# Fused attention and mixture of experts: a new order of the attention periods, fixed PSUM places, the k and q casts cut in two, one score block in fp32

## Chip, core and metric

The kernel is one program on one core of a Trainium2 chip. The metric is the device time of one execution in microseconds (us). The engines are TensorE (PE in the profile; its weight loads are the row PEld), VectorE (DVE), ScalarE (ACT), GpSimd (POOL) and SyncE (SP, which here only starts transfers). Line numbers such as L228 are lines of the kernel before.

## What is computed

Block-causal attention over 8 batches of 8 heads, then a two-level router and 16 experts. All of it is fp32 in and out.

```python
def _attn_ref(q, k, v):                       # q, k, v: (8, 8, 576, 64)
    scores = scale * np.matmul(q, k.transpose(0, 1, 3, 2))
    mask = (pos[:, None] // 64) >= (pos[None, :] // 64)
    scores = np.where(mask, scores, -1000000000.0)
    scores = scores - np.max(scores, axis=-1, keepdims=True)
    attn = np.exp(scores)
    attn = attn / (np.sum(attn, axis=-1, keepdims=True) + 1e-09)
    return np.matmul(attn, v)
...
def _moe_ref(x, w_group, w_expert, w1, w2):   # x: (4608, 512), 4 groups of 4 experts, F = 1024
    g_idx = argmax(x @ w_group); g_w = softmax(x @ w_group)[g_idx]
    e_idx = argmax(x @ w_expert[g_idx]); e_w = softmax(...)[e_idx]
    out = g_w * e_w * (relu(x @ w1[g, e]) @ w2[g, e])
```

## The kernel before

**Attention.** The 64 heads are taken as 32 pairs. A pair's work is a set of tokens, each a few instructions: `K` transposes k and q on PE into a PSUM tile (L157), `k0` and `k1` copy 512 columns each of it to SBUF (`nf`) on ACT; the last 64 columns of k and 128 of q (64 of them padding, "the tails") come through three more transposes (L175) into the free part of another pair's `o` tile, and `j0`, `j1` copy them to `nf` on DVE. `h0`, `h1` cast `nf` to fp32r (the high part), `l0`, `l1` subtract it from `nf` (the low part): both lie in `qk`, k in columns 0 to 575, q in 576 to 1215. A score tile is then three fp32r products, high by high, high q by low k, low q by high k (`PROD`), for each head of the pair. `S0` to `S3` and `S8` are the score tiles of 128, 256, 384, 512 and 576 columns (L228, L218; L234 adds the mask), and the 128-column one lies in the same PSUM tile as the 384-column one, behind it (`S2`). `D` takes the row maximum (DVE, L239), `E` the exponential (ACT, L251), `T` transposes the result back (PE, L157), `t` copies that to `pt` (ACT, L284), `V` multiplies with v in fp32 (PE, L313) and ends with the tail transposes of a later pair, and `v` copies its result out (DVE, L281).

**The software pipeline.** `period(x)` walks the table `ORDER`, in which `S1@0` is token `S1` of pair x, `K@-1` token `K` of pair x+1, and so on; a `d` behind it puts it on DVE, an `a` on ACT. There are 31 such periods and one that walks `END`. The program order of each engine is the order of the tokens; nothing is scheduled afterwards. The router's tokens (`R`, `L`, `n`, `Y`, `M`, `X`, `G`, `Z`) act once in four periods, for the batch that the last four pairs have completed: `L`, `Y`, `X` are PE work (logits and transposes), `n0`, `n1` copies on ACT, `M` and `G` DVE, `Z` indirect DMAs on POOL that write x and its weights. Hooks, given by a token's position or by a step, place the other POOL work.

**PSUM.** Every tile of the attention (transposes, scores, results) is a place of 2 x 512 columns, of which there are four, given in turn to whoever asks next:

```python
def wide(self, name):
    return self.ps2.tile([P, 2, 512], F32, tag="W", name=name)   # pool ps2, bufs=4
```

A period asks for ten of them (`K`, `S1`, `S2`, `S3`, `S8`, `T1` to `T4`, `V`), and one to four more where the router has PE work.

**Experts.** From about 345 us on, the 4608 rows are gathered by expert and go through w1 and w2 in slots. `spill` and `overflow` handle rows beyond the planned slots in a loop whose count (`cnti`) is computed on the chip and is zero for these inputs.

Of the kernel before, what the change touches and what calls it, by code (L numbers as in the profile page):

```python
# [8 lines left out]
F32 = mybir.dt.float32  # L9
# [5 lines left out]
ALU = mybir.AluOpType  # L15
# [37 lines left out]
Z2@7 E3@1 S2@0 D2@0 Z4@8 E2@1 n1@3a E8@1 T1@1 t3@1a t1@1a D0@0 K@-1 Z0@10 Y1@4 S3@0 D3@0 G2@6 R0@3  # L53
k0@-1a V@2 k1@-1a E0@0 E4@0 E5@0 E1@0 M1@4 E6@0 T2@1 S1@0 L0@3 E7@0 t2@1a T4@1 Z3@8 G1@5 S8@0 G0@4 j0@-1d G4@6
j1@-1d t0@1a Z1@9 h0@-1a v@2d L1@2 D1@0 l0@-1d D8@0 n0@3a G3@6 X0@4 X1@5 Y0@3 h1@-1a t4@1a M0@3 l1@-1a T3@0
X2@6
# [11 lines left out]
class Attention:  # L68
    def __init__(self, tc, ctx, inner, q, k, v, consts):
# [9 lines left out]
        self.ps2 = self.psx.enter_context(tc.tile_pool(name="ps2", bufs=4, space=PSUM))  # L79
# [124 lines left out]
    def score(self, i, u):  # L204
# [17 lines left out]
        for u, c0 in ((2, 0), (0, 384)) if u == 2 else ((u, 0),):  # L222
            w = P * (u + 1)
            st = r["s", u] = ps[:, :, c0:c0 + w]
            for x, (hq, hk) in enumerate(self.PROD):
                for z in range(2):
                    p = slice(64 * z, 64 * z + 64)
                    nc.tensor.matmul(st[:, z, :], lhsT=t[p, hq, S + P * u:S + P * u + P], rhs=t[p, hk, 0:w],  # L228
                                     start=x == 0 and c0 == 0, stop=False)
        m = 2 if u == 0 else 1  # L230
# [93 lines left out]
    def start(self, N, order, on_dve, init):  # L324
# [45 lines left out]
    def token(self, i, tok, N):  # L370
# [54 lines left out]
class Router:  # L425
# [187 lines left out]
    def spill(self, at, row, cnti):  # L613
# [32 lines left out]
        V.tensor_copy(cnti[0:1, 0:1], g[0:1, 0, R - 1:R])  # L646
        yield

    def token(self, at, b, tok):
# [61 lines left out]
        elif k == "Z":  # L711
            self.scatter(b, st, j, at.gate(at.now, 3) if j == 3 and not at.closed else None)
# [130 lines left out]
class Moe:  # L843
# [302 lines left out]
    def store(self, s, c, full):  # L1146
# [215 lines left out]
def attention_moe(ctx, tc, q, k, v, w_group, w_expert, w1, w2, out, order=None, on_dve=None):  # L1362
# [16 lines left out]
    with tc.manual_schedule(engines={ET.PE, ET.Activation, ET.DVE, ET.Pool, ET.SP}):  # L1379
# [81 lines left out]
        for _ in run:  # L1461
            pass
# [27 lines left out]
```

## Time and profile before

| what | us |
|---|---|
| median of 3 runs (lowest, highest) | 786.12 (785.64, 787.31) |
| the profiled execution | 785.75 |
| its span, first to last instruction | 784.0 |
| PE busy (share of the span) | 759.1 (97%) |
| DVE busy | 544.7 (69%) |
| ACT busy | 500.4 (64%) |
| POOL busy | 350.2 (45%) |

The profiled execution is 1.75 us longer than its span and lies 0.37 us below the median. Matmuls are pipelined and their ends modelled, so that PE's share is an upper figure. The shares are means over a span whose first 345 us are attention with the router and whose rest is experts: the engines' shares differ between them.

### The profile page before, as it was taken

To read this page: it belongs to the slowest core of one execution; us is meant where nothing else is said; L and a number is where in the kernel's file an instruction comes from. 1 tells how busy PE (TensorE), PEld (TensorE's weight loads), DVE (VectorE), ACT (ScalarE), POOL (GpSimd) and SP (SyncE) were. 2 spreads that over 40 slices of the span, in tenths; PEclk is the share of its full clock that TensorE was granted. 3 is DMA by queue.
4 is the path that set the end of the run, shared out by engine and by line. 5 is a ranking of instruction groups with operands and counts; after the bars stand their busy time and mean duration, and the time that the engine had idled before them with its cause. 6 is when DMAs were issued, how large, how long until landed. Compare 5 with 4: busy or idle time off the path is not lost.

```text
span 784.0 us, 20180 instructions
## 1 busy us (share of the span) xinstructions
PE 759.1 (97%) x7422; PEld 620.5 (79%) x7422; DVE 544.7 (69%) x1153; ACT 500.4 (64%) x1244; POOL 350.2 (45%) x481
## 2 busy tenths in 40 slices
PE   7899999999999999999999999999999999999996
PEld 4677777777777787768888788788988888888874
DVE  5567888888888888885454654754666667777742
ACT  5999999999999998755433433432434545545622
POOL 6444345454545454344143644454551553544212
PEclk9999999999999999999999999999999999999999
DMA  6478464646464636443779979979778897787771
GB/s 137 96 210 237 116 137 109 139 109 139 108 139 108 140 102 159 166 123 117 271 203 225 365 228 237 287 223 219 245 200 234 267 268 188 204 250 231 261 245 42
DMA packets 219108, 146.71 MB, mean 187 GB/s; under 512 B 155558, under 2 KB 186870, under 8 KB 219008
## 3 DMA queue, kind: packets, MB, share of 16 engines
q1 hardware_dynamic: 209920, 120.76, 57.6%
q0 software_dynamic: 9088, 24.64, 9.9%
q8 instruction: 60, 0.98, 0.5%
q14 instruction: 40, 0.33, 0.1%
HBM read 113.46 MB, written 24.59 MB: 176 GB/s over the span
## 4 chain that ended last, share of the span: by engine, by line
PE 80%; ACT 7%; DVE 6%; issue 3%; POOL 2%; DMA 2%; POOLq 0%; SPq 0%; ACTq 0%; DVEq 0%
PE h L1050 18%; PE y L1114 18%; PE o L313 10%; PE s L228 7%; PE tp L157 6%; PE h L1043 4%; PE s L218 3%; ACT pb L251 3%; PE ye L1114 3%; ACT pt L284 3%; PE he L1050 3%; PE y L1122 2%; DVE wl L949 1%; PE y L1133 1%; PE lg L690 1%
## 5 line engine op out<-in xcount | busy, mean ns | idle before, releaser
L1050 PE MATMUL h<-xt,wh 128*128 128x264 f32 (+6 forms) x704 | 156.3, 312 | 2.4 <-DVE xt L1010 2.3
L251 ACT ACTIVATE pb<-s,nm 128x128 f32<-128x128 f32 (+4 forms) x288 | 156.1, 568 | 3.5 <-DVE nm L239 1.6
L949 DVE TENSOR_TENSOR wl<-raw,wh 128x512 fp32r<-128x512 f32 x192 | 147.3, 804 | 8.5 <-ACT wh L948 8.4
L239 DVE TENSOR_REDUCE nm<-s 128x2 f32<-128x768 f32 (+4 forms) x160 | 126.3, 806 | 34.1 <-PE s L234 29.9
L1050 PEld LDWEIGHTS h<-xt,wh 128*128 128x128 f32 x704 | 119.2, 188 | 18.2 <-issue 4.2
L948 ACT CAST wh<-raw 128x512 fp32r<-128x512 f32 x192 | 109.6, 618 | 8.6 <-DMA raw<-in_moe_w_dram 6.0
L284 ACT COPY pt<-tp 128x1024 f32<-128x1024 f32 (+4 forms) x160 | 105.3, 696 | 8.6 <-PE tp L157 6.4
L1050 PE MATMUL h<-xt,wl 128*128 128x264 f32 (+6 forms) x352 | 109.2, 310 | 0.0
L1114 PE MATMUL y<-wh,hring 128*128 128x512 f32 x306 | 106.9, 400 | 0.4 <-ACT ys L1165 0.2
L228 PE MATMUL s<-qk 64*128 64x384 f32 (+3 forms) x768 | 89.9, 343 | 6.4 <-POOL qk L199 3.0
L1167 POOL DMA_INDIRECT out_dram<-ys,ids x40 | 47.0, 1174 | 108.1 <-DVE ys L1163 88.3
L313 PE MATMUL o<-pt,vb 128*64 128x320 f32 (+4 forms) x896 | 93.6, 360 | 0.4 <-DVE tmp L708 0.2
L194 POOL CAST qk<-nf 128x640 fp32r<-128x640 f32 (+1 forms) x63 | 42.7, 701 | 98.1 <-DVE nf L281 71.4
L313 PEld LDWEIGHTS o<-pt,vb 128*64 128x64 f32 x896 | 59.3, 137 | 32.2 <-DVE tmp L708 0.3
L157 PE MATMUL tp<-ident,pb 64*128 64x64 f32 x1600 | 76.3, 226 | 1.6 <-DVE xT L281 1.1
L228 PEld LDWEIGHTS s<-qk 64*128 64x128 f32 x768 | 61.6, 188 | 15.0 <-POOL qk L199 6.1
L157 PEld LDWEIGHTS tp<-ident,pb 64*128 64x128 f32 x1600 | 63.8, 140 | 10.2 <-ACT pb L251 3.9
L982 POOL COPY pl<-xg 128x1024 int16<-128x1024 int16 (+3 forms) x35 | 40.3, 1154 | 62.3 <-DMA xg<-xd,ids 40.6
L1114 PEld LDWEIGHTS y<-wh,hring 128*128 128x128 f32 x306 | 57.4, 188 | 13.1 <-DVE hring L1061 0.5
L1050 PEld LDWEIGHTS h<-xt,wl 128*128 128x128 f32 x352 | 66.2, 188 | 1.2
L251 ACT ACTIVATION_READ_ACCUMULATOR pb<-s,nm 128x1 f32 x288 | 64.1, 223 | 0.0
L199 POOL TENSOR_TENSOR qk<-nf,qk 128x640 fp32r<-128x640 f32 x31 | 61.2, 1975 | 2.6
(255 smaller groups left out, 1324.0 us busy)
## 6 DMA issues: line engine op xcount, KB each, us to landing
raw<-in_moe_w_dram SPq DMA_DIRECT2D x96, 512.0 KB, 4.2
rawq<-in_moe_w_dram SPq DMA_DIRECT2D x24, 512.0 KB, 7.8
natk<-in_k_dram SPq DMA_DIRECT2D x32, 256.0 KB, 3.6
natq<-in_q_dram SPq DMA_DIRECT2D x32, 256.0 KB, 5.5
vb<-in_v_dram SPq DMA_DIRECT2D x64, 128.0 KB, 2.8
wh<-in_moe_w_dram SPq DMA_DIRECT2D x16, 512.0 KB, 5.0
xd<-xns SPq DMA_DIRECT2D x12, 512.0 KB, 3.2
tab<-fill POOLq DMA_DIRECT2D x10, 512.0 KB, 4.1
```

What stands on the lines that cost most here:

```text
L157: self.nc.tensor.transpose(out=out[:, z], in_=src[r], identity=self.c["ident"][r, r])
L199: (eng or self.side(("l", n))).tensor_tensor(out=r["qk"][:, 1, o], in0=r["nf"][:, o], in1=r["qk"][:, 0, o].bitcast(F32), op=ALU.subtract)
L228: nc.tensor.matmul(st[:, z, :], lhsT=t[p, hq, S + P * u:S + P * u + P], rhs=t[p, hk, 0:w], start=x == 0 and c0 == 0, stop=False)
L239: self.nc.vector.tensor_reduce(out=o, in_=r["s", u], op=ALU.max, axis=ax, negate=True)
L251: nc.scalar.activation(reg, src, AF.Exp, bias=r["nm"][:, t:t + 1], accum_out=self.sms[b][:, pr, z, u:u + 1])
L284: return self.nc.scalar.copy(dst, src)
L313: nc.tensor.matmul(o[64 * a:64 * a + 64, hf, c0:c0 + BLK * (b1 - t)], lhsT=r["v"][:, a, j, :], rhs=pt[:, PTJ * j + t:PTJ * j + b1, a, :], ...
L948: nc.scalar.copy(h[:, sl], s["raw", u][:, sl])
L949: nc.vector.tensor_tensor(out=l[:, sl], in0=s["raw", u][:, sl], in1=h[:, sl].bitcast(F32), op=ALU.subtract)
L1050: nc.tensor.matmul(o, lhsT=ww[:, dc, f], rhs=rr[:, dc, t], start=dc == 0 and x == 0, stop=dc == 3 and x == 2)
L1114: nc.tensor.matmul(y[c][0:n], lhsT=hh, rhs=w, start=k == 0 and x == 0, stop=k == 7 and x == 2)
L1167: i = nc.gpsimd.indirect_dma_start(out=self.out, out_offset=bass.IndirectOffsetOnAxis(ap=s["ids"][0:n, c, 0:1], axis=0), in_=ys[0:n], in_o ...
```

## The change

1. **Order.** `ORDER` and `END` are new tables. In `ORDER`, `T1` stands behind `V` rather than ahead of `K`; `L0`, `L1` and `Y0`, `Y1` stand ahead of `V` rather than behind it. In `END` all copies are on ACT, where one was on DVE.
2. **PSUM places.** The pool holds four tiles of one place each, `W0` to `W3`, and a string `SLOTS` of 394 digits says for every wide tile which it takes.
3. **Engines.** `t4` (the copy of `T4`, 128 x 640) and `n0` (a router copy, 128 x 576) go from ACT to DVE. The low part of k goes from DVE to POOL.
4. **Casts.** `h0` casts the 512-column mains of k and q in one instruction, `h1` the two tails; `l1` makes q's main low, `l2` the tails' low, `l0` k's main low. All five are on POOL, but for the first pair, where DVE takes part.
5. **Score block.** The 128-column tile `S0` is two fp32 matmuls straight from `nf`, ahead of the 384-column products in their tile, rather than six fp32r matmuls behind them.
6. **Gates, hooks and tail.** Every `Z` waits for the last row maximum by a one-element copy on POOL (before, one of the five did). Hooks move by position. The last slot's result is scaled on ACT alone (512 columns), not on ACT and DVE by halves; the loop's count is copied by POOL behind everything else, not by DVE earlier.

```diff
 ORDER, ON_DVE = parse("""
-Z2@7 E3@1 S2@0 D2@0 Z4@8 E2@1 n1@3a E8@1 T1@1 t3@1a t1@1a D0@0 K@-1 Z0@10 Y1@4 S3@0 D3@0 G2@6 R0@3
...
+E2@1 Z4@10 X0@4 E3@1 S2@0 Z2@7 t3@1a K@-1 E8@1 G0@5 L0@3 k1@-1a L1@3 D2@0 S3@0 k0@-1a n0@3d Y0@4 D0@0 h0@-1a
...
+SLOTS = """
+3210123130210313201302312032102301320312302103201302312032102301301203210230210132103121301231021320123021320231
...
-        self.ps2 = self.psx.enter_context(tc.tile_pool(name="ps2", bufs=4, space=PSUM))
+        self.ps2 = self.psx.enter_context(tc.tile_pool(name="ps2", bufs=1, space=PSUM))
...
-        return self.ps2.tile([P, 2, 512], F32, tag="W", name=name)
+        return self.ps2.tile([P, 2, 512], F32, tag=f"W{next(self.slots)}", name=name)
...
+    def part(self, t, n):
+
+        if n == "kq":
+            return t[:, 0:2 * S].rearrange("p (n c) -> p n c", c=S)[:, :, 0:512]
+        return t[:, dict(k=slice(0, 512), q=slice(S, S + 512), kt=slice(512, S), qt=slice(S + 512, 2 * S + BLK))[n]]
+
+    def high(self, i, n, eng):
         r = self.rs[i]
+        eng.tensor_copy(self.part(r["qk"][:, 0], n), self.part(r["nf"], n))
+
+    def low(self, i, n, eng):
         r = self.rs[i]
+        eng.tensor_tensor(out=self.part(r["qk"][:, 1], n), in0=self.part(r["nf"], n),
+                          in1=self.part(r["qk"][:, 0], n).bitcast(F32), op=ALU.subtract)
...
-        for u, c0 in ((2, 0), (0, 384)) if u == 2 else ((u, 0),):
-            w = P * (u + 1)
...
+        m = 2 if u == 2 else 1
+        if m == 2:
+            st = r["s", 0] = ps[:, :, 384:512]
+            for z in range(2):
+                p = slice(64 * z, 64 * z + 64)
+                nc.tensor.matmul(st[:, z, :], lhsT=r["nf"][p, S:S + P], rhs=r["nf"][p, 0:P], start=True, stop=False)
...
+        self.last_gate = o[0:1, 0:1]
...
-        self.high(0, 0, nc.vector)
-        self.high(0, 1)
-        self.low(0, 0, nc.vector)
-        self.low(0, 1, nc.vector)
+        self.high(0, "k", nc.vector)
+        self.high(0, "q", nc.gpsimd)
+        self.low(0, "k", nc.vector)
+        self.low(0, "q", nc.vector)
+        for n in ("kt", "qt"):
+            self.high(0, n, nc.gpsimd)
+        for n in ("kt", "qt"):
+            self.low(0, n, nc.gpsimd)
...
         elif k == "h":
-            self.high(i, tok[1])
+            for n in ("kt", "qt") if tok[1] else ("kq",):
+                self.high(i, n, self.side(tok))
         elif k == "l":
-            self.low(i, tok[1])
+            for n in (("k",), ("q",), ("kt", "qt"))[tok[1]]:
+                self.low(i, n, self.side(tok))
...
-            self.scatter(b, st, j, at.gate(at.now, 3) if j == 3 and not at.closed else None)
+            self.scatter(b, st, j, None if at.closed else at.last_gate)
...
-            nc.scalar.activation(ys[0:n, 0:256], y[0:n, 0:256], AF.Copy, scale=cw[0:n])
-            nc.vector.tensor_scalar(out=ys[0:n, 256:512], in0=y[0:n, 256:512], scalar1=cw[0:n], scalar2=None, op0=ALU.mult)
+            nc.scalar.activation(ys[0:n], y[0:n], AF.Copy, scale=cw[0:n])
...
+        nc.gpsimd.tensor_copy(cnti, ro.over)
```

What the tables do to the engines' programs is seen in rows of the program order: line, operation, output and inputs (a digit directly behind a name is the pair or the buffer), size, and a count of equal neighbours.

POOL in a period before, pair 12 in buffer 0 and pair 13 in buffer 1 of `qk` and `nf`: two whole casts and the low part of q, with the router's work between two periods.

```order
L194 CAST qk0_113<-nf0_115 128x576
L194 CAST qk0_113<-nf0_115 128x640
L199 TENSOR_TENSOR qk0_113<-nf0_115,qk0_113 128x640
L812 MEMSET mark_200 1x1
L819 DMA tab_57<-pay0_163,pi0_2026 82560x16
L667 COPY ry1_2141<-rx1_2135 128x2x5x2 x2
L194 CAST qk1_114<-nf1_116 128x576
```

POOL in a period of the changed kernel:

```order
L206 CAST qk1_114<-nf1_116 128x2x512
L210 TENSOR_TENSOR qk1_114<-nf1_116,qk1_114 128x512
L206 CAST qk1_114<-nf1_116 128x64
L206 CAST qk1_114<-nf1_116 128x128
L210 TENSOR_TENSOR qk1_114<-nf1_116,qk1_114 128x64
L210 TENSOR_TENSOR qk1_114<-nf1_116,qk1_114 128x128
L210 TENSOR_TENSOR qk1_114<-nf1_116,qk1_114 128x512
```

The first cast of a pair no longer reads its tails; k's low part is now the last instruction here, behind the tails' four small ones.

PE before, from `S2` of pair 13 to `S3`: the 384-column products, the 128-column ones, masks, `T1`, `K` in two rows, `S3`.

```order
L228 MATMUL s13_2_2704<-qk1_114 128x384 x6
L228 MATMUL s13_2_2704<-qk1_114 128x128 x6
L234 LDWEIGHTS mq_121
L234 MATMUL s13_2_2704<-mk_122,mq_121 128x2x64
L234 LDWEIGHTS mq_121
L234 MATMUL s13_2_2704<-mk_122,mq_121 128x2x64
L157 MATMUL tp12_1_2722<-ident_62,pb0_119 128x64 x8
L157 MATMUL tp14_2734<-ident_62,natk0_117 128x64 x8
L157 MATMUL tp14_2734<-ident_62,natq14_2487 128x64 x8
L228 MATMUL s13_3_2753<-qk1_114 128x512 x6
```

PE in the changed kernel, the same stretch of pair 17:

```order
L238 MATMUL s17_2_3553<-nf1_116 128x128 x2
L244 MATMUL s17_2_3553<-qk1_114 128x384 x6
L250 LDWEIGHTS mq_121
L250 MATMUL s17_2_3553<-mk_122,mq_121 128x2x64
L250 LDWEIGHTS mq_121
L250 MATMUL s17_2_3553<-mk_122,mq_121 128x2x64
L164 MATMUL tp18_3565<-ident_62,natk0_117 128x64 x8
L164 MATMUL tp18_3565<-ident_62,natq18_3322 128x64 x8
L244 MATMUL s17_3_3585<-qk1_114 128x512 x6
```

And further on in the same period of the changed kernel, from the end of `V` (L330) past the tail transposes (L182):

```order
L330 MATMUL o15_3597<-pt15_3285,vb_112 64x64 x2
L182 MATMUL o15_3597<-ident_62,natk0_117 128x64 x3
L164 MATMUL tp16_1_3615<-ident_62,pb0_119 128x64 x8
L164 MATMUL tp16_2_3631<-ident_62,pb0_119 128x64 x16
L244 MATMUL s17_1_3650<-qk1_114 128x256 x6
```

The two fp32 matmuls now lead `S2`, and `T1` has moved from ahead of `K` to behind the tail transposes.

DVE before, from `j0` and `j1` of pair 25 to `S2`'s row maximum of pair 24:

```order
L281 COPY nf0_115<-o21_4892 128x64
L282 TENSOR_SCALAR nf0_115<-o21_4892 128x128
L281 COPY xT5_4687<-o21_4892 128x576
L239 TENSOR_REDUCE nm23_4826<-s23_1_4936 128x2
L199 TENSOR_TENSOR qk0_113<-nf0_115,qk0_113 128x576
L239 TENSOR_REDUCE nm23_4826<-s23_8_4960 128x1
```

DVE in the changed kernel at the same place:

```order
L298 COPY nf0_115<-o21_4878 128x64
L299 TENSOR_SCALAR nf0_115<-o21_4878 128x128
L298 COPY xT5_4662<-o21_4878 128x576
L255 TENSOR_REDUCE nm23_4816<-s23_1_4936 128x2
L298 COPY pt22_4763<-tp22_4_4949 128x2x5x64
L255 TENSOR_REDUCE nm23_4816<-s23_8_4963 128x1
```

Between the two row maxima, the subtraction that made k's low part is gone, and the copy of `T4` stands in its place.

## Rows read from the trace of the kernel before

**Rows 1.** Busy time of each engine (instructions) in five periods, from `V` to `V`.

```profile
core 0: us, PE busy (x) PEld busy (x) DVE busy (x) ACT busy (x) POOL busy (x), PEclk, DMA share, GB/s
38.83:48.15 9.32, 8.81 (x138) 6.88 (x134) 5.58 (x9) 9.12 (x26) 4.39 (x6) 1.00 0.55 144
...
117.05:126.37 9.32, 9.32 (x151) 7.49 (x149) 8.24 (x17) 8.77 (x26) 5.60 (x8) 1.00 0.14 45
126.37:135.69 9.32, 9.32 (x154) 7.49 (x150) 8.03 (x17) 9.18 (x27) 4.49 (x6) 1.00 0.62 151
135.69:145.84 10.15, 9.88 (x164) 7.63 (x160) 8.96 (x27) 9.57 (x27) 4.36 (x5) 1.00 0.56 122
145.84:156.22 10.38, 10.23 (x173) 7.95 (x170) 8.60 (x16) 10.10 (x28) 4.74 (x7) 1.00 0.79 175
```

**Rows 2.** Timeline of PE in the early periods: start, time, instruction, [idle before <-releaser].

```profile
36.55 0.73 PE L228 MATMUL s<-qk 64*128 64x384 f32 x8 [1.00 <-POOL qk L199]
...
41.69 0.28 PE L175 MATMUL o<-ident,natk 64*128 64x64 f32 x2
...
44.78 0.59 PE L228 MATMUL s<-qk 64*128 64x384 f32 x4
45.87 0.72 PE L228 MATMUL s<-qk 64*128 64x384 f32 x8 [0.51 <-POOL qk L199]
46.44 0.23 PE L234 MATMUL s<-mk,mq 64*128 64x128 bf16 x2
...
55.67 0.73 PE L228 MATMUL s<-qk 64*128 64x384 f32 x8 [0.95 <-POOL qk L199]
```

**Rows 3.** Timeline of PE in a period with router work.

```profile
149.92 0.71 PE L690 MATMUL lg<-xT,wcat 64*32 64x288 f32 x16
150.56 0.53 PE L157 MATMUL tp<-ident,pb 64*128 64x64 f32 x10
...
152.00 0.71 PE L157 MATMUL ly<-ident,lt 64*128 64x64 f32 x16
152.55 0.67 PE L157 MATMUL tp<-ident,pb 64*128 64x64 f32 x16
153.03 1.06 PE L228 MATMUL s<-qk 64*128 64x384 f32 x12
153.93 0.23 PE L234 MATMUL s<-mk,mq 64*128 64x128 bf16 x2
```

**Rows 4.** Groups by shape over 20 periods (107 to 303 us): busy, mean ns | idle before.

```profile
L284 ACT COPY pt<-tp 128x640 f32<-128x640 f32 x20 | 14.1, 706 | 0.3 <-PE tp L157 0.3
L199 DVE TENSOR_TENSOR qk<-nf,qk 128x576 fp32r<-128x576 f32 x20 | 15.0, 750 | 0.1
L194 POOL CAST qk<-nf 128x640 fp32r<-128x640 f32 x20 | 14.3, 715 | 0.0
L194 POOL CAST qk<-nf 128x576 fp32r<-128x576 f32 x20 | 13.3, 664 | 53.0 <-DVE nf L281 43.7 <-ACT pb L251 9.2
L228 PE MATMUL s<-qk 64*128 64x128 f32 x120 | 9.0, 253 | 0.0
L313 PE MATMUL o<-pt,vb 128*64 128x128 f32 x80 | 7.8, 273 | 0.0
L284 ACT COPY lt<-lg 128x576 f32<-128x576 f32 x10 | 6.4, 640 | 1.1
L667 POOL COPY ry<-rx 128x20 f32<-128x20 f32 x10 | 1.7, 195 | 19.2 <-DVE rx L664 19.2
```

**Rows 5.** The chain that ended last, 42 to 58 us: start, time, engine and line.

```profile
43.84 1.99 POOL qk L199
```

**Rows 6.** All instructions of line 199: ns min/median/max, first and last start.

```profile
L199 POOL TENSOR_TENSOR qk<-nf,qk x31: 1536/1990/2118, 15.2 to 308.5; 128x640 fp32r<-128x640 f32 x31
```

**Rows 7.** Timeline of all engines at the end of the span (784.0).

```profile
776.97 0.47 ACT L1160 ACTIVATE ys<-y,ids 128x256 f32<-128x256 f32 x1 [4.94 <-PE y L1114]
778.02 0.48 DVE L1161 TENSOR_SCALAR ys<-y,ids 128x256 f32<-128x256 f32 x1 [5.27 <-ACTq L1342]
778.79 0.99 POOL L1167 DMA_INDIRECT out_dram<-ys,ids  x1 [5.81 <-DVE ys L1161]
```

More of the change, by code (lines that the diff above doesn't have):

```diff
@@ L89, in __init__ @@
         self.mk = pfix.tile([P, 2, BLK], BF16, name="mk")
+        self.slots = iter("".join(SLOTS.split()))
         self.lds, self.rs, self.xTs, self.sms = {}, {}, {}, {}
@@ L221, in score @@
             return
-        for u, c0 in ((2, 0), (0, 384)) if u == 2 else ((u, 0),):
-            w = P * (u + 1)
[L224 to L230, printed above, removed]
+        m = 2 if u == 2 else 1
[4 more added lines that the diff above has]
+                nc.tensor.matmul(st[:, z, :], lhsT=r["nf"][p, S:S + P], rhs=r["nf"][p, 0:P], start=True, stop=False)
+        c0, w = 0, P * (u + 1)
+        st = r["s", u] = ps[:, :, 0:w]
+        for x, (hq, hk) in enumerate(self.PROD):
+            for z in range(2):
+                p = slice(64 * z, 64 * z + 64)
+                nc.tensor.matmul(st[:, z, :], lhsT=t[p, hq, S + P * u:S + P * u + P], rhs=t[p, hk, 0:w],
+                                 start=x == 0 and m == 1, stop=False)
+        w += P * (m - 1)
         for z in range(2):
@@ L611, in final, with spill @@
         yield
-    def spill(self, at, row, cnti):
+    def spill(self, at, row):
         nc = self.nc
@@ L645, in spill @@
         nc.sync.dma_start(row, col)
-        V.tensor_copy(cnti[0:1, 0:1], g[0:1, 0, R - 1:R])
+        self.over = g[0:1, 0, R - 1:R]
         yield
@@ L1400, in attention_moe @@
             if x == N - 3:
-                timed = {45: [lambda: moe.index(slots[0]), lambda: moe.getids(slots[0])]}
+                timed = {len(order) - 1: [lambda: moe.index(slots[0]), lambda: moe.getids(slots[0])]}
             if x == N - 2:
@@ L1405, in attention_moe @@
                 z = lambda j, gate: ro.scatter(N // 4 - 3, ro.st[N // 4 - 3], j, gate)
-                timed = {2: [lambda: moe.pump(False)], 8: [lambda: moe.gather_one(at.gate(N - 1, 2))], 20: [lambda: moe.gather_one(at.gate(N - 1, 3))],
-                         29: [lambda: moe.gather_one(at.gate(N - 1, 1))], 32: [lambda: z(4, at.gate(N - 1, 4))]}
+                timed = {2: [lambda: moe.pump(False)],
+                         8: [lambda: moe.gather_one(at.gate(N - 1, 2))],
+                         18: [lambda: moe.gather_one(at.gate(N - 1, 3))],
+                         31: [lambda: moe.gather_one(at.gate(N - 1, 1))],
+                         38: [lambda: z(4, at.gate(N - 1, 4))]}
             if x == 0:
@@ L1434, in attention_moe @@
         }
-        spl = ro.spill(at, rowo, cnti)
+        spl = ro.spill(at, rowo)
         for n in (60, 63, 65, 67, 68, 69):
```

22 lines of the change are left out of this document (9 added, 13 removed).

## The prediction, made before the changed kernel was run

> **What bounds the kernel now.** I read the stretches from one `V` to the next first, because the change lies almost wholly in the attention periods and the shares of the whole span mix these with the experts. Four periods with router work, one batch, last 9.32 + 9.32 + 10.15 + 10.38 = 39.17 us [rows 1]. In them ACT is busy 37.62 us (96%), DVE 33.83 (86%), POOL 19.19 (49%), and PE nearly all of the time, but its ends are modelled. So two engines are full, and it matters which one has real slack.
>
> For PE I went to its timeline in the early periods, which have no router work on PE. There `S2` starts, issues four of its products, and then sits idle for the low part from POOL: 1.00, 0.51 and 0.95 us [rows 2]. From `S2`'s first matmul to its masks 46.44 − 44.78 = 1.66 us pass, while a later period that doesn't wait takes 153.93 − 153.03 = 0.90 [rows 2, 3]. The wait in that 9.32-us period is thus 0.51 by the idle time and 0.76 by the stretch; I take 0.67, so that PE's own work in a plain period is 8.65 us. The chain names what is late there: the subtraction on POOL, 1.99 us [rows 5].
>
> A batch adds router work to PE: two groups of logits at 150.56 − 149.92 = 0.64 us, and 60 transposes (`Y`, `X`) at 152.55 − 152.00 = 0.55 per 16 [rows 3], together 3.34. PE's content of a batch is 4 × 8.65 + 3.34 = 37.94 us, and 39.17 − 37.94 = 1.23 us of waits are left. ACT has 39.17 − 37.62 = 1.55 us that aren't busy. Both are so close to the period that each delays the other now and then.
>
> **Engines.** The copy of `T4` (0.706 us, every period) and `n0` (0.640, once a batch) leave ACT, and the 0.750 of k's low part leaves DVE [rows 4]. Per batch ACT has 37.62 − 4 × 0.706 − 0.64 = 34.16, DVE 33.83 − 3.00 + 2.82 + 0.64 = 34.29. ACT goes from 96% to 87% of the old period, DVE stays near 88%. I price the copies on DVE as on ACT; DVE's nearest row, 0.75 for 576 columns, agrees within some 0.1. So PE is alone at the limit, with 37.7 to 37.9 us of content.
>
> **Score block.** Six fp32r matmuls of 128 columns cost 9.0/20 = 0.45 us of PE's busy time per tile. The same fp32 form, 128 columns in `V`, has four records per period, 7.8/20 = 0.39, for two matmuls [rows 4]. I take −0.06 per period, −0.24 per batch, hence a PE content of 37.70; bounds ±0.2 per period, as these times overlap. The Trainium skill, FP8 and Floating Point Precision, section TensorE Precision Notes, says that true FP32 takes four passes through the array. By it a block of three products at 0.45 would become 0.60, the trace shows two records per fp32 matmul and 0.39, and I go by the trace.
>
> **POOL's chain.** What `S2` waits for is what follows the tail transposes of `V` (41.69): `j0`, `j1`, two casts (0.664 + 0.715 = 1.38), the subtraction of 640 columns (1.99), together 45.87 − 41.69 = 4.18 us, of which 0.81 is neither cast nor subtraction [rows 2, 4]. In the new order the mains are cast, and q's main subtracted, before the tails exist. Behind them come two small casts, two small subtractions and k's 512-column subtraction. Casts rise by 0.8 ns a column (0.664 to 0.715 for 64 more) from a small instruction's 0.195 [rows 4], which makes the two small ones 0.55; the small subtractions are 0.8 at the 2.4 ns a column of the 1.54-us row plus the same base; the large one is 1.54 × 512/640 = 1.23, or 1.59 at the median of 1.99 [rows 6]. Estimate: 0.55 + 0.8 + 1.23 + 0.81 = 3.4 us, 3.75 at the slower rate. I take 1.23, since the subtraction on DVE, 0.75 us long between the same buffers, no longer runs beside it. The Trainium skill, SBUF — State Buffer, section SBUF: two separate sides, says that VectorE with two SBUF inputs and GpSimd take their shared port pair as an exclusive lock. The fastest and median rows of line 199 look like that; by the rule it is 1.23, without it 1.59.
>
> PE now needs k's low part at the third product of `S2`, not the fifth. It comes there 44.78 − 41.69 = 3.09 us after the tail transposes, plus `T1`, moved into this stretch (8 transposes, 0.28), the fp32 pair (0.2) and two products (0.2): 3.8 us. The chain is done 0.4 earlier, or just in time at 3.75. So the wait goes. In the early periods that is between the idle sum, 2.46 us, and 3 × 0.25 more (by the 0.76 against 0.51), 3.2; I take **2.7 us**.
>
> POOL in all grows per period by the second 512-column subtraction, the small ones and the larger casts, 1.6 to 2.2 us, to about 27 of a batch's 39. It is no bound by its sum, only by its place.
>
> **Router batches.** Of the 1.23 us of waits per batch some stem from POOL, some from ACT (full, so its copies come late and hold PSUM places). With ACT relieved and places fixed, between 0 and 1.23 remain. I take 0.75, a little above half, because DVE's load isn't smaller and the row maxima stay in the loop. A batch then takes 37.70 + 0.75 = 38.45, a gain of 0.72, and six batches (the 24 periods from x = 7 to 30) give **4.3 us**. Bounds: nothing, or 1.47 × 6 = 8.8.
>
> **Head, end, tail.** At the start the casts and subtractions that `S2` needs shrink by 64 and 128 columns, worth about 0.3 us by the rates above, while four tail instructions (1.35 by the estimates above) stand ahead of POOL's other start work: 0, bounds ±1.5. `END` is another order with all copies on ACT, for which no row gives a price: 0, bounds ±1.5 (a wait of 1.00 and one of 0.51 either way, as in rows 2). In the tail DVE's half starts 1.05 us after ACT's and the last DMA follows at 778.79 [rows 7]. ACT alone needs about 0.64 (the 576-column copy of rows 4), so the DMA could start some 0.9 earlier. But the loop's count is now copied by POOL after everything, and reading it, hidden before, lies at the end: 0, bounds ±1.2. The gates on `Z` hold POOL until a row maximum is there; that is costed at nothing since POOL is idle 5 us of a period, and it matters only if a gate stands ahead of the casts (below).
>
> **Sum.** −2.7 − 4.3 = −7.0 us. The profiled execution of before is 785.75 (span 784.0), so the changed one is 778.75, span 777. The median stands 0.37 above the profiled one, which gives 779.1.
>
> **Rivals.**
> A. *VectorE becomes the bound.* DVE keeps 34.29 us of work per batch; if the 4.8 to 5.3 us that it isn't busy now (39.17 − 33.83 = 5.34) are waits that stay, the batch lasts 39.1 or more and only the early gain is left: 783.4. For it: `t4` now sits between two row maxima that ACT's exponentials wait for. Against: much of its idle time is waiting for PE.
> B. *Slower: POOL's chain is late.* k's low part stands last on POOL, behind four small instructions and any gated `Z`. If the chain is 1.15 us longer than estimated (0.36 of it the slower rate, the rest a gate or a DMA in its way, as the 0.99 us of a POOL DMA in rows 7), the two boundaries per batch without router transposes between `V` and `S2` wait 1.15 − 0.4 = 0.75 each, the other two about 0.2; with 0.3 of other waits the batch is 37.7 + 1.9 + 0.3 = 39.9, 0.73 more than before. Six batches cost 4.4, the early gain is gone: 790.5. It decides from a chain about 1.0 us longer.
> C. *It doesn't do what it says.* Fixed places replace rotating ones: `T2` may wait for an exponential to free its place, `S1` and `T3` for another, and the 1.23 us come back under other names, the early wait too: about 786.
> D. *The fp32 block is dearer.* At 0.60 against 0.39, 0.21 us in each of 32 periods, 6.7 us are lost: 785.8. This is what the page's four passes would give; the rows speak against it.
>
> **How the numbers follow.** Chances: forecast 0.58, A 0.14, B 0.16, C 0.09, D 0.03. About 0.2% (1.6 us) is what a measurement of this kernel can tell from no change. The forecast and A are faster by more than that (0.72), C and D within it (0.12), B slower (0.16). The forecast's own range is 774.5 to 783 by the bounds of the batches (−8.8 to 0) and the three ±1 to 1.5 terms, which are not all at one end. The range takes in A, C and D and reaches a little below, since the batches' bound is far: 773.5 to 787.5, leaving out B and a few hundredths.
>
> **What the profile after would show.** Right: no idle of PE at `S2` put down to POOL in the early periods, and these periods at 8.6 to 8.8 us; batches near 38.4 us; ACT and DVE both near 34 of it; the large POOL subtractions nearer 1.2 than 1.6 us; the 128-column block at 0.4 us or less of PE time. Wrong: idle at `S2`'s third product behind a late POOL (B); DVE with few gaps and ACT waiting for row maxima (A); PE waiting for exponentials or copies at `T2`, `S1` or `T3` (C); the fp32 rows at 0.6 us per tile (D). The prediction fails mostly if the waits per batch don't shrink, as that term is the largest and was chosen between far ends; a head, `END` or tail that moves by more than 1.5 us would be the second cause.

## The result, and the profile after

The changed kernel is slower: 791.16 us (median of 5 runs, 789.93 to 791.49) against 786.32 of the kernel before in the same comparison (785.64 to 787.94), a ratio of 1.0052, 95% interval [1.0037, 1.0068]. That is 5 us more where 7 less were forecast, and outside the range. The profiled execution took 789.93, its span 788.2.

The loss is found by cutting both spans at the same places: first `V` to fourth, the fifth to the 29th (24 periods, all with router work), from there to the last `V`, to the last matmul, to the end. Windows of the kernel before, columns as in [rows 1]:

```profile
28.69:57.95 29.26, 26.69 (x403) 20.83 (x400) 17.17 (x27) 27.35 (x76) 14.44 (x18) 1.00 0.66 165
...
67.48:303.45 235.97, 233.06 (x3766) 183.56 (x3763) 204.69 (x472) 225.94 (x625) 112.84 (x152) 1.00 0.54 129
303.45:328.60 25.15, 23.36 (x360) 18.10 (x356) 20.43 (x52) 19.89 (x54) 12.86 (x21) 1.00 0.60 176
328.60:776.54 447.94, 443.11 (x2504) 375.31 (x2504) 279.59 (x561) 198.19 (x413) 187.36 (x225) 1.00 0.78 226
776.54:784.00 7.46, 0.39 (x2) 0.00 (x0) 0.48 (x1) 0.47 (x1) 0.99 (x1) 0.79 0.10 37
```

The same windows of the changed kernel:

```profile
28.61:54.58 25.97, 25.97 (x398) 20.23 (x394) 16.90 (x28) 25.00 (x73) 18.75 (x30) 1.00 0.68 182
...
65.08:305.92 240.84, 230.62 (x3718) 179.25 (x3715) 220.90 (x479) 211.73 (x593) 147.27 (x247) 1.00 0.51 126
305.92:328.89 22.97, 22.41 (x345) 17.76 (x341) 18.85 (x50) 19.58 (x54) 14.36 (x26) 1.00 0.67 210
328.89:777.49 448.60, 442.84 (x2504) 375.41 (x2504) 282.56 (x558) 199.12 (x414) 187.22 (x225) 1.00 0.77 224
777.49:788.20 10.71, 0.39 (x2) 0.00 (x0) 0.00 (x0) 0.69 (x1) 1.15 (x2) 0.67 0.08 28
```

The first three periods gain 3.3 us. The 24 router periods lose 4.9 and the tail 3.25. The end of the attention gains 2.2, the experts lose 0.7, and 1.0 goes in the one period between the first two windows (9.53 before, 10.50 after). Part of these two is the same work, moved: 16 of the router's logit matmuls (0.7 us of PE) and 4 of its transposes ran in the end stretch before and run in that one period now. So two losses, 8 us in all, stand against the forecast. Notable in the router window: PE is busy 2.4 us less than before and ACT 14 less, while DVE is busy 16 us more.

One batch of the changed kernel, for the four periods of [rows 1]:

```profile
154.03:162.86 8.83, 8.83 (x143) 7.03 (x139) 8.03 (x16) 7.92 (x25) 7.10 (x12) 1.00 0.13 43
162.86:173.21 10.35, 9.53 (x152) 7.42 (x148) 9.84 (x19) 8.90 (x26) 6.96 (x11) 1.00 0.45 100
173.21:184.37 11.16, 10.35 (x175) 7.62 (x171) 10.04 (x29) 9.93 (x27) 7.04 (x11) 1.00 0.78 187
184.37:194.02 9.65, 9.65 (x167) 7.78 (x163) 8.70 (x18) 8.57 (x25) 4.09 (x9) 1.00 0.59 141
```

The sum is 39.99 against 39.17. The loss sits in the second and third period: PE has idle time there and DVE little. Groups by shape of the changed kernel, 114 to 306 us (19 periods), show what DVE does:

```profile
L210 POOL TENSOR_TENSOR qk<-nf,qk 128x512 fp32r<-128x512 f32 x38 | 48.7, 1281 | 0.2
L229 PE MATMUL s<-qk 128*128 128x288 f32 x114 | 20.2, 312 | 7.6 <-DVE xT L298 7.6
L298 DVE COPY pt<-tp 128x640 f32<-128x640 f32 x19 | 15.5, 814 | 0.0
L792 DVE TENSOR_TENSOR pre<-pre,o 128x16 bf16<-128x16 bf16 x25 | 8.8, 351 | 0.7
L210 POOL TENSOR_TENSOR qk<-nf,qk 128x128 fp32r<-128x128 f32 x19 | 8.7, 456 | 0.0
L760 DVE TENSOR_TENSOR edd<-el,emx 128x20 f32<-128x20 f32 x5 | 8.6, 1713 | 0.2
L210 POOL TENSOR_TENSOR qk<-nf,qk 128x64 fp32r<-128x64 f32 x19 | 6.1, 320 | 0.0
L760 DVE TENSOR_TENSOR gdd<-lgs,gmx 128x20 f32<-128x20 f32 x5 | 0.9, 179 | 0.2
```

Line 760 subtracts 20 columns. For `gdd` it takes 0.18 us, for `edd`, of the same shape, 1.71. The timelines of one such place name the neighbour:

```profile
165.34 1.71 DVE L760 TENSOR_TENSOR edd<-el,emx 128x20 f32<-128x20 f32 x1
165.72 1.29 POOL L210 TENSOR_TENSOR qk<-nf,qk 128x512 fp32r<-128x512 f32 x1
...
167.94 0.74 DVE L298 COPY xT<-o 128x576 f32<-128x576 f32 x1
...
168.74 1.06 PE L229 MATMUL s<-qk 128*128 128x288 f32 x6 [0.82 <-DVE xT L298]
```

DVE's small subtraction ends at 167.05, 0.04 us after POOL's ends at 167.01. Behind it on DVE wait the rest of the router's chain, `j0`, `j1` and `v`'s copy `xT`, and for that copy waits `S8` on PE. In the following period the first of the five additions of line 792 is held in the same way: 1.09 us instead of 0.17, beside the subtraction at 174.62; the mean of the five, 0.351, hides that it is one. This gave the theory for the experiments: **POOL's early subtraction of q's main part, which the change put where the router's chain runs on DVE, holds those operations**. Rivals: DVE's load by `t4` and `n0`; the fixed places (`S8` takes the place of `o`). For the tail the theory was the late count.

The tail of the changed kernel, answering to [rows 7]:

```profile
777.92 0.69 ACT L1183 ACTIVATE ys<-y,ids 128x512 f32<-128x512 f32 x1 [4.94 <-PE y L1137]
778.88 0.99 POOL L1189 DMA_INDIRECT out_dram<-ys,ids  x1 [4.95 <-ACT ys L1183]
779.85 0.18 POOL L1488 CAST cnti<-fin 1x1 int32<-1x1 f32 x1
```

The last DMA starts 778.88 − 777.49 = 1.39 us after the start of the last matmul (before: 778.79 − 776.54 = 2.25), yet the end is 8.35 us behind the start of the count's copy.

### The profile page after: what moved, and what is told of

The parts are those of the page before. It is cut to its first block, busy times and chain, and to the rows that moved or that the text cites. A ratio compares the mean times of both kernels' runs of the same rounds, so it can differ in the third digit from the quotient of the medians.

```text
span 788.2 us, 20081 instructions
## 1 busy us (share of the span) xinstructions
PE 755.1 (96%) x7358; PEld 615.0 (78%) x7358; DVE 560.3 (71%) x1154; ACT 483.9 (61%) x1210; POOL 397.0 (50%) x610
## 4 chain that ended last, share of the span: by engine, by line
PE 75%; DVE 12%; ACT 5%; issue 2%; DMA 2%; POOL 1%; SPq 0%; DVEq 0%; POOLq 0%; ACTq 0%
PE h L1073 19%; PE y L1137 18%; PE o L330 9%; PE tp L164 8%; PE s L244 6%; PE s L229 4%; PE h L1066 3%; DVE nm L255 2%; PE y L1145 2%; DVE wl L972 2%; PE ye L1137 1%; DVE pre L792 1%; ACT pb L268 1%; PE he L1073 1%; PE xn L164 1%
## 5 line engine op out<-in xcount | busy, mean ns | idle before, releaser
L268 ACT ACTIVATE pb<-s,nm 128x384 f32<-128x384 f32 (+4 forms) x288 | 155.8, 557 | 19.7 <-DVE nm L255 17.5
L210 POOL TENSOR_TENSOR qk<-nf,qk 128x512 fp32r<-128x512 f32 (+2 forms) x126 | 101.6, 827 | 0.5
L330 PE MATMUL o<-pt,vb 128*64 128x320 f32 (+4 forms) x896 | 93.6, 360 | 0.0
L301 ACT COPY pt<-tp 128x1024 f32<-128x1024 f32 (+4 forms) x130 | 85.3, 708 | 12.0 <-PE tp L164 9.9
L206 POOL CAST qk<-nf 128x128 fp32r<-128x128 f32 (+3 forms) x96 | 49.2, 530 | 74.5 <-ACT nf L301 54.6
L330 PEld LDWEIGHTS o<-pt,vb 128*64 128x64 f32 x896 | 59.3, 137 | 31.8 <-issue 0.2
L244 PE MATMUL s<-qk 64*128 64x384 f32 (+2 forms) x576 | 77.1, 368 | 1.5 <-ACT nf L301 0.5
L164 PE MATMUL tp<-ident,pb 64*128 64x64 f32 x1600 | 73.4, 227 | 4.1 <-ACT pb L268 2.7
L164 PEld LDWEIGHTS tp<-ident,pb 64*128 64x128 f32 x1600 | 61.4, 139 | 10.6 <-issue 4.8
L1137 PE MATMUL y<-wl,hring 128*128 128x512 f32 x153 | 60.6, 396 | 0.0
L268 ACT ACTIVATION_READ_ACCUMULATOR pb<-s,nm 128x1 f32 x288 | 60.2, 209 | 0.0
```

Of the source, the lines that this page charges most:

```text
L164: self.nc.tensor.transpose(out=out[:, z], in_=src[r], identity=self.c["ident"][r, r])
L206: eng.tensor_copy(self.part(r["qk"][:, 0], n), self.part(r["nf"], n))
L210: eng.tensor_tensor(out=self.part(r["qk"][:, 1], n), in0=self.part(r["nf"], n), in1=self.part(r["qk"][:, 0], n).bitcast(F32), op=ALU.subtract)
L268: nc.scalar.activation(reg, src, AF.Exp, bias=r["nm"][:, t:t + 1], accum_out=self.sms[b][:, pr, z, u:u + 1])
L301: return self.nc.scalar.copy(dst, src)
L330: nc.tensor.matmul(o[64 * a:64 * a + 64, hf, c0:c0 + BLK * (b1 - t)], lhsT=r["v"][:, a, j, :], rhs=pt[:, PTJ * j + t:PTJ * j + b1, a, :], ...
```

## The experiments

The runs were made in five groups (1 to 4, 5 to 8, 9 to 12, 13 and 14, 15), each on one chip together with the kernel before, and a ratio is to that kernel on the same chip. The chips differ, so ratios of different groups are compared only with care, and stretches of the profiled executions stand beside them.

**1. The count early.**

```diff
-        self.over = g[0:1, 0, R - 1:R]
+        V.tensor_copy(cnti[0:1, 0:1], g[0:1, 0, R - 1:R])
...
-        nc.gpsimd.tensor_copy(cnti, ro.over)
```

> The changed kernel, with the loop's count copied by DVE inside the spill again (as before) and not by POOL behind everything. Theory: the end is longer by 3.2 us because every engine reads the count and walks the loop's branches only after POOL's last copy; then the stretch from the last matmul to the end falls from 10.7 to 7.5 us or somewhat less (ACT alone stores), and the time is 787 to 788. Rival: the store on ACT alone, or the last DMA's landing, makes the end; then the stretch stays near 10.7 and the time near 791.

Measured: from the last matmul to the end 7.72 us, not 10.71. The time was 793.56, ratio 1.0058 [1.0040, 1.0076]: the stretch fell as the theory says. The total missed the 787 to 788 expected; the profiled execution lost time elsewhere (the head 1.5, the router periods 1.8, the end of the attention 3.4, for which see the last section). The DMA started 787.01 − 784.52 = 2.49 us after the last matmul here, as late as before: the early DMA and the late count come together. The last stretch here:

```profile
784.52:792.24 7.72, 0.39 (x2) 0.00 (x0) 0.00 (x0) 0.69 (x1) 0.99 (x1) 0.81 0.11 39
```

**2. The kernel before with the count late**, the same edit the other way round.

> The kernel before with the count copied by POOL behind everything, nothing else changed (the store stays split over ACT and DVE). Theory: the end grows by 3 to 4 us, 789.5 to 790.5. Rival (the store or chance): 786.3, unchanged.

Measured: 791.37, ratio 1.0046 [1.0031, 1.0061], 3.6 us by the ratio and 2.9 by the medians. The last stretch is 10.49 against 7.46:

```profile
777.92:788.41 10.49, 0.39 (x2) 0.00 (x0) 0.48 (x1) 0.47 (x1) 1.15 (x2) 0.64 0.07 27
```

The count's place alone makes the tail's loss; the store on ACT alone doesn't. The DMA started 779.62 − 777.92 = 1.70 us after the last matmul here, earlier than before with the store split as before.

**3. POOL's subtraction of q in halves.**

```diff
+        for c in (slice(0, 256), slice(256, 512)) if n == "q" else (slice(None),):
+            eng.tensor_tensor(out=o[:, c], in0=s[:, c], in1=h[:, c], op=ALU.subtract)
```

> The changed kernel, with the subtraction that makes q's main low on POOL cut into two of 256 columns. Theory (DVE's router operations with two SBUF inputs can't run while POOL's subtraction does, and stand 1.5 and 1.0 us in two of four periods): a held operation waits half as long, the 1.71-us operation of line 760 falls to about 1.0, the five of line 792 lose about 0.5 in sum, a batch falls from 40.0 to 39.0 to 39.5 us, and the time to 786 to 789. Rival (DVE's load by the two copies moved to it): 791, with the same batches. Rival (the fixed PSUM places): 791.

Measured: 791.45, ratio 1.0040 [1.0024, 1.0055], above the 786 to 789 expected. Groups by shape of this kernel, where line 763 is the next operation of the chain (0.18 us in the changed kernel):

```profile
L763 DVE SCALAR_TENSOR_TENSOR esc<-edd,desc 128x20 f32<-128x20 f32 x5 | 3.3, 653 | 0.2
L761 DVE TENSOR_TENSOR edd<-el,emx 128x20 f32<-128x20 f32 x5 | 3.0, 608 | 0.2
L765 DVE TENSOR_TENSOR eoh<-esc,em 128x20 f32<-128x20 f32 x5 | 2.1, 427 | 0.2
L764 DVE TENSOR_REDUCE em<-esc 128x5 f32<-128x20 f32 x5 | 0.9, 176 | 0.2
```

One wait of 1.53 became three of 0.43, 0.47 and 0.25 (line 765, also 0.18 otherwise), 1.15 in sum. The reduction of line 764 between the last two, which has one input, wasn't held, though POOL's second half ran beside it:

```profile
165.74 1.43 POOL L212 TENSOR_TENSOR qk<-nf,qk 128x256 fp32r<-128x256 f32 x2
166.57 0.18 DVE L764 TENSOR_REDUCE em<-esc 128x5 f32<-128x20 f32 x1
```

The 24 router periods took 239.26 against 242.65 of run 1 on the same chip (240.84 in the first profile of the changed kernel). The additions of line 792 (0.351) didn't improve, against the expectation: two of the five are held, each about half as long.

**4. The router's chain later on DVE**: in `ORDER`, `G1@5` and `G2@6` behind `D8@0`.

> The changed kernel, with the router's tokens G1 and G2 (VectorE) moved from ahead of the tail copies and v's copy to behind the last row maximum D8; no work is added or removed. Theory: the chain leaves the stretch in which POOL subtracts, v's copy is no longer late, S8 doesn't wait for it, and a batch falls from 40.0 to about 38.5 to 39.0: 784 to 787. Rival (DVE's load): the sum of DVE's work is the same, so the batches stay near 40, 790 to 791. Rival (the places): S8 still waits for its place, 790 to 791.

Measured: 813.76, ratio 1.0313 [1.0292, 1.0335], a plain miss. Line 760 is back at 0.18 us and `S8` doesn't wait any more, so the holding and its consequence went together. But ACT's exponential in the chain now waits 9.3 us for DVE in 186 us of these periods, the next score tile on PE 7.1 for ACT, and the clock granted to PE falls to 0.94 of full speed in one of the periods. The place of the chain has a price of its own; this run says nothing on the sum.

**5. The changed kernel again.** No edit.

> The changed kernel once more, unaltered, as the level for the others on the same chip: a ratio of 1.005 to before as on the first chip, or up to 1.007 if this chip shows the lower clock more often.

Measured: 795.36, ratio 1.0091 [1.0059, 1.0123], above the 1.007 expected at most; the 24 router periods 243.14 us, the tail 10.63. Runs 6 to 8 were made on the same chip. Two profiles of the same kernel thus differ by 2.3 us in the router periods (240.84 and 243.14), so smaller differences of this stretch between runs say little.

**6. POOL's subtraction of q replaced by a fill**, which reads nothing. The kernel leaves out q's low part in these 512 columns.

```diff
+        if n == "q" and i > 0:
+            eng.memset(self.part(r["qk"][:, 1], n).bitcast(F32), 0.0)
+            return
```

> The changed kernel, with POOL's subtraction of q's main low part replaced by a fill with zeros (it leaves out q's low part in columns 0 to 511, so the scores lose precision): POOL's instruction stays in its place but reads no SBUF and is shorter. Theory (POOL's subtraction holds DVE's operations with two SBUF inputs): line 760 falls to 0.18 us and line 792 to 0.17 each, v's copy comes 1.0 to 1.5 us earlier in two of four periods, a batch falls from 40.0 to 38.0 to 38.5, six batches give 9 to 12 us against the changed kernel. Rival (DVE's load by t4 and n0, or the fixed places): less than 3 us.

Measured: 784.46, ratio 0.9954 [0.9930, 0.9977], 10.9 us below the changed kernel, within the 9 to 12 expected. Its router periods, and groups of this kernel:

```profile
64.19:297.30 233.11, 230.79 (x3718) 179.87 (x3714) 207.63 (x479) 211.80 (x593) 129.44 (x246) 1.00 0.53 130
L232 PE MATMUL s<-qk 128*128 128x288 f32 x114 | 20.2, 312 | 0.0
L795 DVE TENSOR_TENSOR pre<-pre,o 128x16 bf16<-128x16 bf16 x25 | 4.2, 167 | 0.7
L763 DVE TENSOR_TENSOR edd<-el,emx 128x20 f32<-128x20 f32 x5 | 0.9, 180 | 0.2
```

`S8` waits for nothing (7.6 us before). In one place the fill ran on POOL from 170.84 to 171.36 and the five additions on DVE from 171.03 on, 0.17 each: this instruction on POOL, which doesn't read SBUF, doesn't hold them. The router periods took 233.11 us, 10 less than in run 5 and less than the kernel before (235.97).

**7. `t4` and `n0` back on ACT** (`t4@1a`, `n0@3a`).

> The changed kernel with t4 and n0 back on ACT. Theory of the hold: DVE is still held 2.4 us per batch, but has 3.9 us less to do, so part of the delay of v's copy stays (0 to 0.5 us at S8, where it is 0.8 now): a batch falls by 0 to 0.8 us, the time by 0 to 5. Rival (the two copies make DVE the bound): S8 no longer waits for v's copy, a batch falls to 38.5, the time by 9 us against the changed kernel.

Measured: 797.32, ratio 1.0096 [1.0066, 1.0125]; no gain. `S8` still waits 7.7 us for `xT`, `edd` takes 1.86. DVE's load by the copies isn't the cause.

**8. The places in turn**, `bufs=4` and one tag as before.

> The changed kernel with the four PSUM places given in turn, as before, and not by the string. Rival (fixed places make S8 wait for v's copy): the wait of S8 goes and the time falls by 5 us or more. Theory: S8 then waits for another tile or others wait, no gain; within 2 us of the changed kernel or slower by up to 10.

Measured: 796.02, ratio 1.0094 [1.0061, 1.0127]. `S8` waits 7.6 us for `xT` as with the string. The fixed places aren't the cause either, and bring nothing here.

**9. The fp32 block undone**: six fp32r matmuls behind the 384-column ones, as before.

> The changed kernel, with the 128-column score block as six fp32r matmuls from qk behind the 384-column ones again. Forecast of the prediction: the block is dearer by 0.06 us a period on PE (0.04 by the starts of the matmuls in the changed trace), 1 to 2 us in all if PE is the bound, and nothing to be seen where DVE is: within 2 us of the changed kernel (a ratio near 1.008 to before). Rival D (the fp32 block costs 0.21 a period): 6 us faster than the changed kernel.

Measured: 799.07, ratio 1.0115 [1.0087, 1.0143], not told apart from the changed kernel on the other chip (1.0091); the router periods 243.65 against 243.14. The experts, which the edit doesn't touch, took 453.5 us of this profiled execution against 448.2 in run 5. There is no sign of a gain of 6 us. Run 15 does this again where PE waits less.

**10. Fill and early count together.**

> The two suspected costs taken away together: POOL's subtraction of q's main low part is a fill with zeros (the scores lose precision), and the count is copied early by DVE. Theory: the two add, 0.9954 and another 3 us, so the time is 7 us or 0.9% below before (0.990 to 0.993), which is what the prediction gave for the whole change. Rival (they share a cause, such as the clock at the end of attention): no lower than 0.995.

Measured: 781.54, ratio 0.9905 [0.9889, 0.9921]. The forecast was 779.1 of 786.12, a ratio of 0.9911. Without the two costs the time falls by about what was forecast. Part of that agreement is chance: q's low part is left out here too, and the profiled spans of this run and of the kernel before, from different chips, are 4.2 us apart (779.8 and 784.0), as the head is 1.2 and the one period 1.0 longer. Its windows (three early periods, 24 router periods):

```profile
29.90:55.86 25.96, 25.96 (x397) 20.33 (x393) 16.89 (x28) 25.02 (x73) 16.58 (x30) 1.00 0.68 182
66.37:299.03 232.66, 230.74 (x3719) 179.83 (x3715) 207.51 (x479) 211.86 (x593) 129.30 (x246) 1.00 0.53 130
```

**11. q's low part on DVE, count early** (`l1@-1d`).

> The changed kernel with the count copied early and with the subtraction of q's main low part on DVE instead of POOL (exact). Theory: nothing holds the router's chain, but DVE has 0.7 us more in every period, 2.7 per batch against 2.4 of holding taken away; the periods without router work on DVE grow by 0 to 0.3, the two held ones shrink by 0.3 to 0.8, so a batch goes from 40.4 to 39.5 to 40.4 and the time is 1.000 to 1.005 of before. Rival (DVE's load is the bound): a batch above 41, 1.012 or more.

Measured: 788.15, ratio 0.9990 [0.9978, 1.0003], a little better than expected; the router periods 237.12. The 512-column subtraction takes 0.675 us on DVE.

**12. Quarters, count early.**

> The changed kernel with the count copied early and POOL's subtraction of q's main low part cut into four of 128 columns (exact). Theory: a held operation of DVE waits at most some 0.4 us at a time, and several can be held one after the other; a batch goes from 40.4 to 39.2 to 39.8, with the 3 us of the count 0.998 to 1.002 of before. Rival (holding is by share, not by instruction): the same as the changed kernel with the count early, 1.006.

Measured: 792.06, ratio 1.0049 [1.0031, 1.0066], a miss. Groups of this kernel:

```profile
L763 DVE SCALAR_TENSOR_TENSOR esc<-edd,desc 128x20 f32<-128x20 f32 x5 | 7.3, 1466 | 0.2
L761 DVE TENSOR_TENSOR edd<-el,emx 128x20 f32<-128x20 f32 x5 | 1.6, 322 | 0.2
```

One operation of DVE gets in after a short wait, the next is held until the third of POOL's four has ended. In sum it is 1.43 us, about as much as by one long instruction. The router periods took 240.7 us against 237.12 of run 11 on the same chip. Cutting is no cure.

**13. q's low part on DVE in the two held periods only, count early.**

```diff
-                self.low(i, n, self.side(tok))
+                self.low(i, n, self.nc.vector if n == "q" and i >= 9 and i % 4 in (1, 2) else self.side(tok))
```

> The changed kernel with the count copied early, and the subtraction of q's main low part on DVE only in the two periods of a batch in which it holds the router's chain, on POOL in the other two (exact). Theory: DVE has 0.68 us more in those two periods and 1.0 to 1.5 us less of holding, the other two stay as in the changed kernel (9.66 and 8.82); a batch is 38.6 to 39.0, against 39.2 with q on DVE in all periods and 38.5 without any q part; the time is 0.995 to 0.998 of before. Rival (a load on DVE costs wherever it stands): as with q on DVE everywhere, 0.999.

Measured: 780.74, ratio 0.9932 [0.9905, 0.9958]: faster than both kernels and than expected, with the whole computation; the router periods took 233.98. A batch of it (second and third period were 10.35 and 11.16):

```profile
151.85:160.66 8.81, 8.81 (x143) 7.03 (x140) 8.03 (x16) 7.92 (x25) 7.10 (x12) 1.00 0.13 43
160.66:170.11 9.45, 9.45 (x151) 7.41 (x148) 8.89 (x20) 8.91 (x26) 5.68 (x10) 1.00 0.50 111
170.11:180.92 10.81, 10.36 (x174) 7.63 (x170) 9.62 (x30) 9.95 (x27) 5.78 (x10) 1.00 0.87 208
180.92:190.58 9.66, 9.66 (x167) 7.79 (x163) 8.70 (x18) 8.59 (x25) 4.11 (x9) 1.00 0.52 123
```

**14. As 11, with `t4` and `n0` on ACT.**

> The kernel with q's low part on DVE in all periods and the count early, now with t4 and n0 back on ACT. If DVE's load (the two copies) is a second cause that the holding covered, the waits of S8 for v's copy go and the time falls by 3 us or more, to 0.995 or less; ACT then has 38.2 us per batch. If the copies cost nothing beside the holding, ACT becomes the bound and the time is 0.999 to 1.006.

Measured: 785.91, ratio 0.9984 [0.9970, 0.9998], against 0.9990 with the copies on DVE; the router periods 236.85 against 237.12. The copies cost and bring nothing that can be told here.

**15. As 13, with the block in fp32r, and 13 once more on the same chip.**

> The best kernel so far (q's low part on DVE in the two held periods, the count early), with the 128-column score block as six fp32r matmuls again. There PE has fewer waits than in the changed kernel, so the block's price should show. Forecast of the prediction: 0.06 us a period dearer, about 2 us over the attention, so some 2 us slower than the same kernel with the fp32 block in this call. Rival D (fp32 costs 0.21 a period more): 6 us faster. If the block's products, which need the low parts, bring back a wait at the score tile, slower by more than 3 us.

> The best kernel so far once more, on the same chip as the one without the fp32 block: 0.993 of before as in its first run, 0.990 to 0.996.

Measured: 787.06, ratio 0.9959 [0.9944, 0.9973], and 785.36, ratio 0.9952 [0.9934, 0.9970]. The fp32 block is worth 0 to 2 us: 1.7 by the medians, with overlapping intervals. With it the three early periods are 25.97 against 26.26, so 0.1 us a period, and the router periods 235.26 against 235.99.

## Why the prediction was wrong

**Early periods: right.** −2.7 was forecast, 25.97 − 29.26 = −3.3 measured. The idle time of `S2` behind POOL in [rows 2] is gone (0.2 us in all are left between 28 and 58 us), and the periods are 8.5 to 8.8 us. The estimates of POOL's chain were met: the large subtraction 1.28 (1.23 taken), the two small ones 0.32 + 0.46 (0.8), the small casts 0.24 + 0.29 (0.55).

**Router batches: the step that failed.** −4.3 was forecast, +4.9 measured. The step gave DVE 34.29 us a batch from durations of [rows 4, 6] and asked of POOL only whether its chain is in time for `S2` ("no bound by its sum, only by its place"). DVE was busy 36.60, 2.3 more, and holding accounts for as much: 1.53 at line 760 and 0.92 at the first addition of line 792 per batch. Without it, in run 10, DVE was busy 207.51 / 6 = 34.6 a batch, close to the 34.29. In the kernel before POOL waited for the tail copies at that point (the 43.7 us at its first cast in [rows 4]), so the router's chain, ahead of these copies on DVE, met no subtraction: `edd` took 0.18 there too. The split removed that wait, which was counted as gain alone. Runs 6 and 10 show it in full, and with the holding away the same term is 232.66 − 235.97 = −3.3, near the −4.3 forecast. The gates of `Z`, costed at nothing, have a part that no run varied alone: in the held period the gate's copy and its DMA (164.37 to 165.70) stand on POOL just ahead of the subtraction and so set when it starts.

The prediction had the mechanism in hand. It used [rows 6] and the Trainium skill, SBUF — State Buffer, section SBUF: two separate sides, to ask what slows POOL's instruction, and never which DVE instructions POOL's new one would block. By that section of the Trainium skill either side can block, and the other waits for the whole instruction. The runs agree that DVE is blocked: 1.71 instead of 0.18 us beside a subtraction, 0.17 beside a fill that reads nothing. What the records leave open is told in the last section.

**Tail: the second step that failed.** 0 ± 1.2 was forecast, +3.25 measured, and runs 1 and 2 show that the count's place makes it. It had been seen that the read lies at the end, but its price was bounded by a guess. The DMA did start 0.9 earlier, as worked out, but not for the reason given: with ACT alone and the count early (run 1) it started 2.49 us after the last matmul, with the split store and the count late (run 2) 1.70, against 2.25 before. So it was the late count that brought it forward; the store on ACT alone added 0.3 to that (1.39 against 1.70) and nothing without it.

**Small terms.** `t4` takes 0.814 and `n0` 0.758 on DVE (0.706 and 0.640 were taken), 0.55 more a batch; runs 7 and 14, without the copies on DVE, were not measurably faster. ACT's 35.33 a batch is 1.2 above the sum, which I didn't follow up. The fp32 block was priced rightly: the −0.06 lies within what run 15 shows, and the four passes of the Trainium skill, FP8 and Floating Point Precision, section TensorE Precision Notes (rival D), would have given 6.7 us the other way. `END` measured −2.2 in the profiled execution, outside its ±1.5, but part of that is the router work that moved out of it into the one period, which grew by 1.0 and for which the prediction had no term; the two together are −1.2. (Of the four tokens `L0`, `L1` and `Y0` passed `V`; `Y1` stood ahead of it before.) That stretch is moreover between 23.0 and 27.2 us in the runs above with the same `END`, so its size stays open.

**The rivals.** B gave the time (790.5) by a mechanism that didn't occur: POOL's chain was not late. A was right that DVE became what the others wait for, wrong that its load did it (runs 7, 14). C is refuted by run 8 as far as the places go. D is refuted by run 15.

## What to carry to other kernels

Work that is moved onto an idle engine must be checked against what runs beside it at its new time, not only against what waits for its result: here a 1.3-us subtraction on GpSimd held operations of VectorE with two inputs in SBUF, and a wait in the old order had kept them apart. Where the same work can run on either engine, choose by period, as run 13 does. A value that steers a loop should be there before the last work of the program ends, and a gain of a microsecond in front of the end says nothing until the whole tail is read.

## What the runs showed of the hardware

In the changed kernel's batch shown above, an operation of VectorE with two inputs in SBUF that met GpSimd's subtraction ended 0.02 to 0.05 us behind it: `edd` at 167.05 against 167.01, the addition of line 792 at 175.91 against 175.89. Operations with one input weren't held: 0.18 us for the reduction in run 3, and in the changed kernel 0.81 for `t4`'s copy from PSUM, as long as on average, at 169.20, while GpSimd subtracted k from 169.03 to 170.30.

Which of the two came first doesn't explain it by the records. `edd` started at 165.34 and would have been done by 165.52, yet it was held by a subtraction recorded from 165.72 on; until 165.70 GpSimd was at an indirect DMA. In run 6 the same operation beside the same kind of DMA, with a fill behind it, took 0.18. In run 3 `edd` waited 0.43 and ended at 165.85, inside the first half (165.74 to 166.49). GpSimd's times are rough in a profile, so what held `edd` ahead of the subtraction stays open.

Cutting GpSimd's instruction doesn't shorten the holding reliably: 1.53 us in one piece, 0.43 + 0.47 + 0.25 on three operations in halves, 0.14 + 1.29 on two in quarters.

In run 1 the end of the attention took 26.37 us instead of 22.97, for two reasons. PE was idle longer, and then the clock granted to it fell to half (1.2 GHz). Windows of that kernel:

```profile
329.00:330.00 1.00, 0.47 (x6) 0.23 (x5) 0.12 (x1) 0.00 (x0) 1.00 (x1) 1.00 0.62 223
330.00:331.00 1.00, 0.42 (x8) 0.25 (x7) 0.46 (x1) 0.61 (x1) 0.02 (x1) 1.00 0.86 308
331.00:332.00 1.00, 0.53 (x9) 0.42 (x10) 1.00 (x3) 1.00 (x3) 0.00 (x0) 0.99 0.03 6
332.00:333.00 1.00, 1.00 (x6) 1.00 (x7) 0.42 (x1) 0.54 (x1) 0.00 (x0) 0.50 0.93 346
```

PE was about half idle for 3 us ahead of the fall, and then the 16 transposes of line 1043 took 3.60 us. In run 5, the changed kernel again, PE was idle as long at this place and the clock stayed; in its first profile PE was busy 2.46 of the 3 us. Rows of run 1 (one), run 5 (two) and the first profile (one), in this order:

```profile
331.94 3.60 PE L1043 MATMUL xpe<-ident,xge 128*128 128x128 f32 x16
328.37:331.37 3.00, 1.42 (x24) 0.90 (x22) 1.55 (x4) 1.55 (x2) 1.04 (x1) 1.00 0.50 179
331.37 1.94 PE L1043 MATMUL xpe<-ident,xge 128*128 128x128 f32 x16
324.02:327.02 3.00, 2.46 (x72) 2.24 (x67) 2.58 (x5) 3.00 (x6) 2.27 (x4) 1.00 0.59 201
```

The end of the attention was 26.37, 24.76 and 22.97 us. Up to the transposes of line 1043 the stretch was 1.8 us longer in run 5 than in the first profile (22.90 against 21.10, run 1: 22.84), and where the clock fell it cost another 1.7 (3.60 − 1.94). It fell in the profiles of runs 1, 6, 7, 11, 12 and in that of run 13 made again, and there this stretch took 26.4 to 27.2 us; at full clock it took 23.0 to 25.5. That is more than several of the terms of the sum.
